# Reading 128 weight rows early, through GpSimd's queue, on 32 partitions instead of 128

## The chip, the cores and the metric

One core of one Trainium2 chip runs the program. The metric is the time of one execution on the device, in microseconds (us), as the median of three runs. One more execution was taken with the hardware profiler; its rows are shown below.

## What is computed

A decode step of one transformer block with adaptive layer norm, for a batch of 4 and a model width of 512, all in float32:

```python
x = A_x
mod = (_silu(c) @ w_mod).reshape(c.shape[0], 6, 1, -1)
sa, ca, ga, sb, cb, gb = (mod[:, 0], mod[:, 1], mod[:, 2], mod[:, 3], mod[:, 4], mod[:, 5])
h = _layernorm(x, axis=-1) * (1 + ca) + sa
x = x + ga * _A_ref(h, A_k_cache, A_v_cache, A_wq, A_wo)
h = _layernorm(x, axis=-1) * (1 + cb) + sb
x = x + gb * _B_ref(h, B_w1, B_w3, B_w2)
return x
```

`_A_ref` is attention of 32 query heads and 8 key/value heads over the last 2048 cached positions, `_B_ref` a gated feed-forward layer with 1792 inner columns. The change is about `gb`, the last of the six gates: four batch rows of `_silu(c)`, 512 long, times the last 512 columns of `w_mod`, a matrix of 512 rows.

## The kernel before

Everything that is read once from memory, some 101 MB, is streamed into two large SBUF buffers `KV[0]` and `KV[1]` and a smaller one, `WP`. Nearly all of it is loaded by one queue, SyncE's (SP): the helper `load` at L89 issues a transfer of 128 partitions, and before a buffer is overwritten SP waits for the product that last read it. The first transfers are `T0` (the condition vector `c` and the weights of the first two gates) and the caches of the first head group; ScalarE's queue adds two more (`t1_in` and the 4 rows of `x_in`). Then a loop runs over four pairs of head groups, each with its scores, softmax, values and output projection.

After the loop comes a straight part, the "post" block. The weights of three gates (`wm_in`), the first feed-forward weights (`f1_in`, `f2_in`), the weights of the last gate (`gb_in`, 1 MB, four chunks of 128 rows side by side) and the second feed-forward weights (`w2_in`, in six pieces of 1 MB, 1 MB, 512, 512, 256 and 256 KB) follow one another in SP's queue in this order, with a semaphore for each. TensorE takes them up in the same order and waits for each semaphore. A product of a 128-row chunk with the four batch rows is one call of `mm` at L255; its result is 4 rows by 512 columns in a PSUM bank. For `gb` four chunks go to four groups of rows of the bank `bM`, ScalarE copies the bank to `gb_sb`, and a product with the 0/1 matrix `same` adds the four groups. The last piece of `w2_in` is multiplied last; VectorE then forms `yt` (L488) and `y` (L490), and SP writes `out` (L492).

GpSimd does little: it clears a few tiles at the start (L128 to L139) and later passes semaphores on.

Of the kernel before, what the change touches and what calls it, by code (L numbers as in the profile page):

```python
# [5 lines left out]
AF = mybir.ActivationFunctionType  # L6
# [4 lines left out]
B, D, HQ, G, SK, DH, W, FF = 4, 512, 32, 8, 8192, 128, 2048, 1792  # L11
P = 128
# [2 lines left out]
EPS = 1e-5  # L15
CHUNKS = [(j, c) for c in range(4) for j in range(4) if c < 2 or j < 3]
HEAD = 8
W2_CUTS = [0, 4, 8, 10, 12, 13, 14]
PAIRS = G // 2

# [20 lines left out]
        return (self.sem, self.n)  # L41


def block_kernel(nc, x_in, t0_in, t1_in, kv_in, w_in, wm_in, f1_in, f2_in, gb_in, w2_in, out):
    T, v, s, gp, S = nc.tensor, nc.vector, nc.scalar, nc.gpsimd, nc.sync

    def sems(names):
        return [nc.alloc_semaphore(n) for n in names.split()]

    def sb(name, cols, rows=P):  # L50
        return nc.alloc_sbuf_tensor(name, (rows, cols), F32).ap()

    def bank(name):
        return nc.alloc_psum_tensor(name, (P, 512), F32).ap()

    (first,) = sems("first")
    A = Queue(nc, s, "act")
    V = Queue(nc, v, "dve")
    L = Queue(nc, gp, "pool")
    dx, dt0, dt1, dkv, dk, dva, dvb, dwo, dm, df1, df2a, df2b, dgb = sems("dx dt0 dt1 dkv dk dva dvb dwo dm df1 df2a df2b dgb")  # L60
    dw = sems(" ".join(f"dw{i}" for i in range(len(W2_CUTS) - 1)))
    z_ok, q_ok, p_ok, k_ok, va_ok, vb_ok, pt_ok, o_ok, ot_ok = sems("z_ok q_ok p_ok k_ok va_ok vb_ok pt_ok o_ok ot_ok")
    s_done, q_done, qt_done, pp_done, o_done, x_done, a_done, pe, last = sems("s_done q_done qt_done pp_done o_done x_done a_done pe last")
# [1 line left out]

    KV = [sb("KV0", 16384), sb("KV1", 16384)]
    WP = sb("WP", 8192)
    T0 = KV[1][:, : 16 + 4096]
    x_sb = sb("x_sb", 512, B)
    ident, same, eps = sb("ident", P), sb("same", B), sb("eps", 1)  # L70
    sc, e1, e2 = sb("sc", 16), sb("e1", 16), sb("e2", 16)
    hT, h2T = sb("hT", 16), sb("h2T", 16)
    Z = sb("Z", B * 28)
    q_sb, p_sb, o_sb, a_sb, y_sb, g_sb, u_sb, gb_sb = [sb(n, 512) for n in "q_sb p_sb o_sb a_sb y_sb g_sb u_sb gb_sb".split()]
# [10 lines left out]
    bS, bQ, bT, bP, bO, bX, bA, bM = [bank(n) for n in "bS bQ bT bP bO bX bA bM".split()]  # L85


    def load(dst, src, sem):
        S.dma_start(dst, src).then_inc(sem, 16)  # L89

    load(T0, t0_in, dt0)
    s.dma_start(WP[:, 4096:], t1_in).then_inc(dt1, 16)
# [27 lines left out]
    S.wait_ge(x_done, G)  # L120
    load(KV[1][:, :3072], f2_in[:, :3072], df2a)
    load(KV[1][:, 3072:6144], f2_in[:, 3072:], df2b)
    load(KV[1][:, 6144:8192], gb_in, dgb)
    for a, b, sem in zip(W2_CUTS[:-1], W2_CUTS[1:], dw):
        load(KV[1][:, 8192 + a * 512 : 8192 + b * 512], w2_in[:, a * 512 : b * 512], sem)


    l_eps = L.op(gp.memset(eps, EPS))  # L128
    t = L.op(gp.memset(ident, 0.0))
    L.wait(t)  # L130
# [48 lines left out]
    v_same = V.op(v.tensor_reduce(same, ident.rearrange("p (j i) -> p i j", i=32)[:, :B, :], axis=AX.X, op=ALU.add))  # L179

    A.wait((dt0, 16))
    t = A.op(s.activation(e1, T0[:, :16], AF.Exp, scale=-1.0))
    V.wait(t)
    t = V.op(v.tensor_scalar(e2, e1, 1.0, None, op0=ALU.add))
    V.wait(t)
    t = V.op(v.reciprocal(e2, e2))
    V.wait(t, (dt0, 16))
    t_sc = V.op(v.tensor_mul(sc, T0[:, :16], e2))  # L188

    A.wait((pe, 1))  # L190
    t_sa = A.op(s.copy(sa_sb, bM[32 : 32 + B, :]))
# [1 line left out]
    t = V.op(v.scalar_tensor_tensor(xs, bM[:B, :], 1.0, xc, op0=ALU.add, op1=ALU.mult))  # L193
# [60 lines left out]
    def mm(o, lhsT, rhs, start=True, stop=True):  # L254
        return T.matmul(o, lhsT, rhs, start=start, stop=stop, skip_group_check=True)  # L255
# [46 lines left out]
    T.wait_ge(V.sem, t_sc[1])  # L302
    for k in range(4):
        for i in range(2):
            ins = mm(bM[32 * i : 32 * i + B, :], sc[:, k * B : (k + 1) * B], T0[:, 16 + (2 * k + i) * 512 : 16 + (2 * k + i + 1) * 512], k == 0, k == 3)
    ins.then_inc(pe, 1)
    T.wait_ge(V.sem, t_h[1])
    for k in range(4):
        ins = T.transpose(bT[:, k * B : (k + 1) * B], h[:, k * P : (k + 1) * P], ident[:B, :B])
# [71 lines left out]
    for k in range(4):  # L381
        for i in range(3):
            at = (3 * k + i) * 512
            ins = mm(bX[32 * i : 32 * i + B, :], sc[:, k * B : (k + 1) * B], KV[0][:, at : at + 512], k == 0, k == 3)
# [3 lines left out]

    V.wait((pe, 3), t_ga)
    t = V.op(v.tensor_mul(ag, bM[:B, :], ga_sb))  # L390
    V.wait(t)
    t_x1 = V.op(v.scalar_tensor_tensor(x1, ag, 1.0, x_sb, op0=ALU.mult, op1=ALU.add, accum_out=st2[:, 0:1]))
    t_ss, t_r0, t_xc = stats(x1, t_x1, st2)
# [10 lines left out]
    for k in range(4):  # L404
        ins = T.transpose(bT[:, k * B : (k + 1) * B], h[:, k * P : (k + 1) * P], ident[:B, :B])
# [4 lines left out]
    def view(t_):  # L410
        return t_.rearrange("p (c j i) -> p c j i", c=4, j=4)
# [4 lines left out]
    for k in range(4):  # L416
        for j in range(4):
            at = 6144 + k * 2048 + j * 512
            ins = mm(bQ[32 * j : 32 * j + B, :], h2T[:, k * B : (k + 1) * B], KV[0][:, at : at + 512], k == 0, k == 3)
# [3 lines left out]
    for k in range(4):  # L423
# [5 lines left out]
        for j in range(3):  # L429
            at = k * 1536 + j * 512  # L430
            ins = mm(bA[32 * j : 32 * j + B, :], h2T[:, k * B : (k + 1) * B], KV[1][:, at : at + 512], k == 0, k == 3)
    ins.then_inc(pe, 1)
    A.wait((pe, 7))
    t = A.op(s.activation(view(eT), view(bP)[:, :, :, :B], AF.Exp, scale=-1.0))
    V.wait(t)
    t = V.op(v.tensor_scalar(dT, eT, 1.0, None, op0=ALU.add))
    V.wait(t)
    t = V.op(v.reciprocal(rT, dT))
# [7 lines left out]
    for c in range(4):  # L446
        ins = T.transpose(bS[:, c * P : c * P + 96], u_sb[:96, c * P : (c + 1) * P], ident[:96, :96])
# [3 lines left out]


    T.wait_ge(dgb, 16)
    for k in range(4):
        ins = mm(bM[32 * k : 32 * k + B, :], sc[:, k * B : (k + 1) * B], KV[1][:, 6144 + 512 * k : 6144 + 512 * (k + 1)])
    ins.then_inc(pe, 1)
    A.wait((pe, 10))
    t_gb = A.op(s.copy(gb_sb, bM))
    T.wait_ge(V.sem, t_hid[1])
    hw = view(hidT)  # L460
    w2 = KV[1][:, 8192 : 8192 + 14 * 512].rearrange("p (n m) -> p n m", n=14)
    for i in range(len(W2_CUTS) - 1):
        T.wait_ge(dw[i], 16)
        for n in range(W2_CUTS[i], W2_CUTS[i + 1]):
            jj, c = CHUNKS[n]
            if n < HEAD:
                ins = mm(bO[32 * (n % 4) : 32 * (n % 4) + B, :], hw[:, c, jj, :], w2[:, n, :], n < 4, n >= HEAD - 4)
                continue
            for j in range(4):
                ins = mm(bX[32 * j : 32 * j + B, :P], hw[:, c, jj, :], w2[:, n, j * P : (j + 1) * P], n == HEAD, n == 13)  # L470
        if i == 0:
            T.wait_ge(A.sem, t_gb[1])
            for j in range(4):
                ins = mm(bT[32 * j : 32 * j + B, :P], same, gb_sb[:, j * P : (j + 1) * P])
# [13 lines left out]
    t = V.op(v.tensor_mul(yt, bX[:, :P], gbJ))  # L488
# [8 lines left out]
def _layout(i):  # L497
    import numpy as np

    def a(t):  # L500
        return np.ascontiguousarray(t)

    k = i["A_k_cache"][:, :, SK - W :, :].reshape(B, G, NT, 512, DH)
    v = i["A_v_cache"][:, :, SK - W :, :].reshape(B, G, NT, 4, P, DH)
    k = k.transpose(1, 4, 2, 0, 3).reshape(G, P, 8192)
    v = v.transpose(1, 4, 2, 0, 3, 5).reshape(G, P, 8192)
    wm = i["w_mod"].reshape(4, P, 6, 512).transpose(1, 0, 2, 3)
    c = i["c"].reshape(B, 4, P).transpose(2, 1, 0).reshape(P, 16)
    wq = i["A_wq"].reshape(4, P, G, 512).transpose(2, 1, 0, 3).reshape(G, P, 2048)
    wo = i["A_wo"].reshape(G, R, P, D).transpose(0, 2, 1, 3).reshape(G, P, 2048)  # L510
    pairs = [[wo[2 * p], wo[2 * p + 1]] + ([wq[2 * p + 2], wq[2 * p + 3]] if p < 3 else [wo[6], wo[7]]) for p in range(4)]
    w1 = i["B_w1"].reshape(4, P, FF).transpose(1, 0, 2)
    w3 = i["B_w3"].reshape(4, P, FF).transpose(1, 0, 2)
    w2 = i["B_w2"].reshape(14, P, D)
    return {
        "x_in": a(i["A_x"].reshape(B, D)),
        "t0_in": np.concatenate([c, wm[:, :, 1::-1].reshape(P, 4096)], 1),
        "t1_in": np.concatenate([wq[0], wq[1]], 1),
        "kv_in": np.concatenate([k, v], 2),
        "w_in": np.stack([np.concatenate(p, 1) for p in pairs]),  # L520
        "wm_in": a(wm[:, :, 2:5]).reshape(P, 6144),
        "f1_in": np.concatenate([w1, w3[:, :, 1536:]], 2).reshape(P, 8192),
        "f2_in": a(w3[:, :, :1536]).reshape(P, 6144),
        "gb_in": a(wm[:, :, 5]).reshape(P, 2048),
        "w2_in": a(np.stack([w2[4 * j + c_] for j, c_ in CHUNKS], 1)).reshape(P, 14 * D),
    }

# [14 lines left out]
```

## Time and profile before

| what | value |
|---|---|
| median of three runs | 243.21 us (242.92 to 243.47) |
| the profiled execution's own time | 243.12 us |
| its span, first to last instruction | 241.8 us |
| mean granted TensorE clock, share of full speed | 0.852 |
| moved by DMA | 101.33 MB, mean 419 GB/s |
| TensorE busy | 136.2 us, 56% of the span |

The profiled execution lies 0.09 us under the median. Its own time is 1.3 us more than its span, which is what lies around the first and the last instruction. Busy shares are means over stages with different limits, so the table alone does not say what a stage waits for.

### The profile page before, as it was taken

To read this page: it belongs to the slowest core of one execution; us is meant where nothing else is said; L and a number is where in the kernel's file an instruction comes from. 1 tells how busy PE (TensorE), PEld (TensorE's weight loads), DVE (VectorE), ACT (ScalarE), POOL (GpSimd) and SP (SyncE) were. 2 spreads that over 40 slices of the span, in tenths; PEclk is the share of its full clock that TensorE was granted. 3 is DMA by queue.
4 is the path that set the end of the run, shared out by engine and by line. 5 is a ranking of instruction groups with operands and counts; after the bars stand their busy time and mean duration, and the time that the engine had idled before them with its cause. 6 is when DMAs were issued, how large, how long until landed. Compare 5 with 4: busy or idle time off the path is not lost. (4 is left out here: it accounts for less than half of the span.)

```text
span 241.8 us, 2271 instructions
## 1 busy us (share of the span) xinstructions
PE 136.2 (56%) x940; PEld 37.3 (15%) x940; DVE 38.6 (16%) x126; ACT 25.1 (10%) x54; POOL 1.7 (1%) x14
## 2 busy tenths in 40 slices
PE   3004677817660387276723772667237768665964
PEld 0000121201210012112200121112001222111211
DVE  3003202202200022022000220220002222124122
ACT  2002002100120002001100020001001201123110
POOL 2000000000000000000000000000000000000000
PEclk9999959967996579987985798879858997995999
DMA  7998989899989898999898989998989999999992
GB/s 266 451 500 369 499 371 488 379 417 445 493 379 488 369 499 381 407 428 510 369 499 369 499 369 423 434 510 369 499 350 442 442 400 440 453 431 396 418 411 106
DMA packets 4044, 101.33 MB, mean 419 GB/s; under 512 B 452, under 2 KB 580, under 8 KB 1096
## 3 DMA queue, kind: packets, MB, share of 16 engines
q1 hardware_dynamic: 3888, 99.17, 95.6%
q10 hardware_dynamic: 152, 2.11, 2.1%
q8 instruction: 3, 0.05, 0.1%
q14 instruction: 1, 0.01, 0.0%
HBM read 101.20 MB, written 0.07 MB: 419 GB/s over the span
## 5 line engine op out<-in xcount | busy, mean ns | idle before, releaser
L255 PE MATMUL bS<-KV,Z 128*16 128x512 f32 x256 | 42.5, 824 | 38.8 <-PEq L258 38.8
L255 PE MATMUL bO<-KV,pT 128*16 128x512 f32 x256 | 31.9, 642 | 0.5
L255 PEld LDWEIGHTS bS<-KV,Z 128*16 128x16 f32 x256 | 9.1, 122 | 66.6 <-issue 66.6
L218 DVE TENSOR_REDUCE MX<-bS 128x1 f32<-128x512 f32 x8 | 5.5, 691 | 79.6 <-PE bS L255 79.6
L255 PE MATMUL bM<-KV,sc 128*4 128x512 f32 x24 | 7.3, 835 | 16.6 <-DVE sc L188 16.6
L367 ACT ACTIVATE p_sb<-bS,NB 128x512 f32<-128x512 f32 x8 | 5.5, 687 | 101.2 <-ACTq L358 101.2
L276 PE MATMUL bP<-ident,p_sb 128*128 128x128 f32 x32 | 5.0, 280 | 17.3 <-PEq L258 17.3
L255 PE MATMUL bA<-WP,oT 128*4 128x512 f32 x64 | 10.4, 728 | 5.2 <-PEq L258 5.2
L255 PEld LDWEIGHTS bO<-KV,pT 128*16 128x16 f32 x256 | 8.1, 105 | 22.9 <-issue 22.9
L372 ACT ACTIVATE o_sb<-bO,LB 128x512 f32<-128x512 f32 x8 | 5.5, 687 | 48.7 <-ACTq L358 48.7
L255 PE MATMUL bQ<-WP,hT 128*4 128x512 f32 x64 | 9.2, 648 | 0.6 <-DVE hT L197 0.6
L276 PE MATMUL bX<-ident,o_sb 128*128 128x128 f32 x32 | 5.0, 280 | 7.9 <-PEq L258 7.9
L244 DVE TENSOR_REDUCE oT<-bX 128x16 f32<-128x64 f32 x8 | 1.8, 224 | 44.0 <-PE bX L276 44.0
L276 PE MATMUL bT<-ident,q_sb 128*128 128x128 f32 x32 | 5.5, 298 | 3.6 <-PEq L258 3.6
L276 PEld LDWEIGHTS bP<-ident,p_sb 128*128 128x128 f32 x32 | 3.4, 140 | 24.4 <-issue 24.4
L276 PEld LDWEIGHTS bX<-ident,o_sb 128*128 128x128 f32 x32 | 3.4, 141 | 15.0 <-issue 15.0
L227 DVE COPY pT<-bP 128x256 f32<-128x256 f32 x8 | 3.4, 424 | 13.7 <-PE bP L276 13.7
L255 PE MATMUL bQ<-KV,h2T 128*4 128x512 f32 x32 | 5.3, 831 | 0.3 <-DVE h2T L408 0.3
L276 PEld LDWEIGHTS bT<-ident,q_sb 128*128 128x128 f32 x32 | 3.7, 150 | 8.3 <-issue 8.0
L255 PEld LDWEIGHTS bM<-KV,sc 128*4 128x4 f32 x24 | 1.0, 106 | 22.6 <-DVE sc L188 18.2
L255 PE MATMUL bX<-KV,sc 128*4 128x512 f32 x24 | 4.4, 592 | 0.0
L202 DVE TENSOR_REDUCE Z<-bT 128x16 f32<-128x64 f32 x8 | 1.8, 224 | 15.4 <-PE bT L276 15.1
(101 smaller groups left out, 68.0 us busy)
## 6 DMA issues: line engine op xcount, KB each, us to landing
WP<-w_in SPq DMA_DIRECT2D x3, 4096.0 KB, 18.9
KV<-kv_in SPq DMA_DIRECT2D x1, 4096.0 KB, 24.1
KV<-f_in SPq DMA_DIRECT2D x1, 4096.0 KB, 25.9
KV<-kv_in SPq DMA_DIRECT2D x1, 3072.0 KB, 30.9
KV<-wm_in SPq DMA_DIRECT2D x1, 3072.0 KB, 16.5
KV<-f_in SPq DMA_DIRECT2D x2, 1536.0 KB, 17.2
KV<-t_in SPq DMA_DIRECT2D x1, 2056.0 KB, 12.3
WP<-t_in ACTq DMA_DIRECT2D x1, 2048.0 KB, 12.5
```

Source lines behind the costliest of these rows:

```text
L202: v.tensor_reduce(Z.rearrange("p (b i) -> p b i", b=B)[:, :, 12 : 12 + R], bT.rearrange("p (r k i) -> p i r k", r=R, k=4)[:, :B], axis=AX. ...
L218: t = V.op(v.reduce_max(MX[:, 0:1], bS, axis=AX.X))
L227: v.tensor_copy(pT.rearrange("p (t b c r) -> p c b t r", t=NT, b=B, c=4), bP.rearrange("p (c b i) -> p c b i", c=4, b=B)[:, :, :, :16].rea ...
L244: V.op(v.tensor_reduce(oT.rearrange("p (r b) -> p r b", r=R), diag, axis=AX.X, op=ALU.add), ot_ok)
L255: return T.matmul(o, lhsT, rhs, start=start, stop=stop, skip_group_check=True)
L276: ins = T.transpose(dst[:, c * P : (c + 1) * P], src[:, c * P : (c + 1) * P], ident)
L367: A.op(s.activation(p_sb, bS, AF.Exp, bias=NB[:, 0:1], accum_out=SM[:, 0:1]), p_ok)
L372: A.op(s.mul(o_sb, bO, LB[:, 0:1]), o_ok)
```

## The change

The last of the four chunks of `gb`'s weights, rows 384 to 511 of `w_mod`, leaves SP's transfer `gb_in`, which shrinks from 2048 to 1536 columns. It gets an array of its own, `gc_in`, in which the 128 weight rows lie as 32 rows of 2048 columns (four weight rows side by side, `SUB = 4`), in eight groups of four with a row of zeros behind each group. GpSimd's queue loads these 32 rows at the start of the program into a tile `GC` of 80 partitions that it has cleared before: 16 rows to partitions 16 to 31 and 16 rows to partitions 64 to 79. One transfer ahead of these two and one behind them move 16 rows of 512 bytes each into a tile `GZ` that nothing reads. The condition vector gets 16 more columns that match the new layout, so that `T0` and the tiles `sc`, `e1` and `e2` grow from 16 to 32 columns.

TensorE multiplies `GC` after the product `ag`, with four calls of `mm` over 80 partitions that write the four row groups of `bM`; later the remaining three chunks are added to three of these groups.

```diff
+SUB = 4
+BANDS = [16, 64]
+ROWS = [p for at in BANDS for p in range(at, at + 16)]
+C_IN = 16 + 4 * SUB
+W2_AT = 6144 + 1536
...
+    GC, GZ = sb("GC", SUB * 512, 80), sb("GZ", P, 96)
...
-    load(KV[1][:, 6144:8192], gb_in, dgb)
+    load(KV[1][:, 6144:7680], gb_in, dgb)
...
+    t = L.op(gp.memset(GC, 0.0))
+    L.wait(t)
+    gp.dma_start(GZ[:16], gc_in[:4, :4, :P]).then_inc(dgc, 16)
+    for e, at in enumerate(BANDS):
+        gp.dma_start(GC[at : at + 16], gc_in[4 * e : 4 * e + 4, :4]).then_inc(dgc, 16)
+    gp.dma_start(GZ[80:], gc_in[:4, :4, :P]).then_inc(dgc, 16)
...
     t = V.op(v.tensor_mul(ag, bM[:B, :], ga_sb))
+    T.wait_ge(V.sem, t[1])
+    T.wait_ge(dgc, 64)
+    for m in range(SUB):
+        mm(bM[32 * m : 32 * m + B, :], sc[:80, 16 + m * B : 16 + (m + 1) * B], GC[:, m * 512 : (m + 1) * 512], True, m == 3)
...
-    for k in range(4):
-        ins = mm(bM[32 * k : 32 * k + B, :], sc[:, k * B : (k + 1) * B], KV[1][:, 6144 + 512 * k : 6144 + 512 * (k + 1)])
+    for k in range(3):
+        ins = mm(bM[32 * k : 32 * k + B, :], sc[:, k * B : (k + 1) * B], KV[1][:, 6144 + 512 * k : 6144 + 512 * (k + 1)], False, True)
...
+    gc = np.zeros((8, 5, SUB * 512), c.dtype)
+    gc[:, :4] = i["w_mod"][384:, 5 * 512 :].reshape(SUB, 32, 512).transpose(1, 0, 2).reshape(8, 4, SUB * 512)
...
-        "gb_in": a(wm[:, :, 5]).reshape(P, 2048),
+        "gb_in": a(wm[:, :3, 5]).reshape(P, 1536),
+        "gc_in": gc,
```

On SP's queue, near its end, these transfers stood one behind the other; a row gives the line, the tile, the source, and partitions by columns:

```order
L89 DMA KV<-f_in 128x8192
L89 DMA KV<-f_in 128x3072 [waits x_done]
L89 DMA KV<-f_in 128x3072
L89 DMA KV<-gb_in 128x2048
L89 DMA KV<-w_in 128x2048 x2
L89 DMA KV<-w_in 128x1024 x2
L89 DMA KV<-w_in 128x512 x2
```

and now these stand there:

```order
L95 DMA KV<-f_in 128x8192
L95 DMA KV<-f_in 128x3072 [waits x_done]
L95 DMA KV<-f_in 128x3072
L95 DMA KV<-gb_in 128x1536
L95 DMA KV<-w_in 128x2048 x2
L95 DMA KV<-w_in 128x1024 x2
L95 DMA KV<-w_in 128x512 x2
```

Only the size of `gb_in` differs; no transfer of SP's moved past another. On GpSimd, at the start of the program, the change puts a memset and four transfers ahead of the old memsets:

```order
L556 MEMSET const-uint8-127 128x1
L134 MEMSET GC 80x2048 [waits barrier_Pool_Activation_PE_DVE_SP_gather]
L136 DMA GZ<-gc_in 16x1x128 [waits pool]
L138 DMA GC<-gc_in 16x1x2048 x2
L139 DMA GZ<-gc_in 16x1x128
L140 MEMSET eps 128x1
L141 MEMSET ident 128x128
L144 ISA [waits pool]
L144 AFFINE_SELECT ident<-ident 128x128
```

Before, the memset of `eps` was the first of GpSimd's work; all nine later instructions now come behind the four transfers. On TensorE, behind the products for the three gates, this stood (a row is a product or a transpose, with the tiles and the rows by columns of its result):

```order
L255 MATMUL bX<-KV,sc 4x512 [waits dm]
L255 MATMUL bX<-KV,sc 4x512 x11
L405 MATMUL bT<-ident,h 128x4 [waits dve]
L405 MATMUL bT<-ident,h 128x4 x3
L255 MATMUL bQ<-KV,h2T 4x512 [waits df1,dve]
```

and now this stands there:

```order
L267 MATMUL bX<-KV,sc 4x512 [waits dm]
L267 MATMUL bX<-KV,sc 4x512 x11
L267 MATMUL bM<-GC,sc 4x512 [waits dgc,dve]
L267 MATMUL bM<-GC,sc 4x512 x3
L421 MATMUL bT<-ident,h 128x4 [waits dve]
L421 MATMUL bT<-ident,h 128x4 x3
L267 MATMUL bQ<-KV,h2T 4x512 [waits df1,dve]
```

Four products came in ahead of the transposes of `h`; the four products of `bM` that wait for `dgb` further down became three.

## Rows read from the trace of the kernel before

**Rows 1.** The page, DMA and bytes in 40 slices, and its queues.

```profile
DMA  7998989899989898999898989998989999999992
GB/s 266 451 500 369 499 371 488 379 417 445 493 379 488 369 499 381 407 428 510 369 499 369 499 369 423 434 510 369 499 350 442 442 400 440 453 431 396 418 411 106
q1 hardware_dynamic: 3888, 99.17, 95.6%
q8 instruction: 3, 0.05, 0.1%
```

**Rows 2.** The chain that ended last: start us, length us, what.

```profile
212.29 26.78 DMA KV<-w_in
239.06 0.04 issue
239.11 0.45 PE bX L255 x8
...
239.57 0.30 DVE yt L488
...
239.90 0.29 DVE y L490
```

**Rows 3.** Windows at the end; the last two numbers are DMA share, GB/s.

```profile
227.80:230.27 2.47, 2.47 (x19) 0.73 (x16) 1.12 (x4) 0.22 (x1) 0.00 (x0) 1.00 1.01 421
...
235.28:236.57 1.29, 1.04 (x8) 0.11 (x8) 0.14 (x1) 0.00 (x0) 0.00 (x0) 1.00 1.01 386
236.57:237.20 0.63, 0.58 (x20) 0.35 (x23) 0.55 (x1) 0.00 (x0) 0.00 (x0) 1.00 0.76 267
237.20:238.02 0.82, 0.53 (x20) 0.24 (x20) 0.00 (x0) 0.00 (x0) 0.00 (x0) 1.00 0.18 67
238.02:238.40 0.38, 0.38 (x16) 0.17 (x8) 0.00 (x0) 0.00 (x0) 0.00 (x0) 1.00 0.12 49
238.40:238.65 0.25, 0.25 (x12) 0.11 (x8) 0.00 (x0) 0.00 (x0) 0.00 (x0) 1.00 0.11 41
238.65:239.06 0.41, 0.24 (x8) 0.00 (x0) 0.00 (x0) 0.00 (x0) 0.00 (x0) 1.00 0.00 0
```

**Rows 4.** DMA issues: KB each, median us from issue to landing.

```profile
KV<-w_in SPq DMA_DIRECT2D x2, 1024.0 KB, 23.9
KV<-gb_in SPq DMA_DIRECT2D x1, 1024.0 KB, 20.8
```

**Rows 5.** Timeline of SP's queue around the issue of gb_in.

```profile
209.44 0.43 SPq L89 DMA_DIRECT2D KV<-gb_in  x1
```

**Rows 6.** Timeline of the start: GpSimd's memsets, and what TensorE then waits for.

```profile
1.43 0.52 POOL L135 MEMSET y_sb<- 128x512 f32 x1
2.53 2.08 PE L255 MATMUL bA<-y_sb 128*128 128x512 f32 x2 [2.53 <-POOL x1J L139]
21.25 1.02 PE L255 MATMUL bM<-KV,sc 128*4 128x512 f32 x2 [16.65 <-DVE sc L188]
```

**Rows 7.** Timeline from 215 us on, where the four products come in.

```profile
216.03 0.68 DVE L390 TENSOR_TENSOR ag<-bM,ga_sb 4x512 f32<-4x512 f32 x1 [5.26 <-ACT ga_sb L387]
220.26 0.58 PE L405 MATMUL bT<-ident,h 4*128 4x4 f32 x4 [4.98 <-DVE h L398]
228.09 0.42 PEld L276 LDWEIGHTS bP<-ident,g_sb 128*128 128x128 f32 x4 [0.86 <-DMA KV<-f_in]
231.86 1.04 PE L255 MATMUL bM<-KV,sc 128*4 128x512 f32 x8
235.32 1.04 PE L255 MATMUL bO<-KV,hidT 128*4 128x512 f32 x8 [1.16 <-DMA KV<-w_in]
```

More of the change, by code (lines that the diff above doesn't have):

```diff
@@ L41, in op, with block_kernel @@
         return (self.sem, self.n)
-def block_kernel(nc, x_in, t0_in, t1_in, kv_in, w_in, wm_in, f1_in, f2_in, gb_in, w2_in, out):
+def block_kernel(nc, x_in, t0_in, t1_in, kv_in, w_in, wm_in, f1_in, f2_in, gb_in, gc_in, w2_in, out):
     T, v, s, gp, S = nc.tensor, nc.vector, nc.scalar, nc.gpsimd, nc.sync
@@ L59, in block_kernel @@
     L = Queue(nc, gp, "pool")
-    dx, dt0, dt1, dkv, dk, dva, dvb, dwo, dm, df1, df2a, df2b, dgb = sems("dx dt0 dt1 dkv dk dva dvb dwo dm df1 df2a df2b dgb")
+    dx, dt0, dt1, dkv, dk, dva, dvb, dwo, dm, df1, df2a, df2b, dgb, dgc = sems("dx dt0 dt1 dkv dk dva dvb dwo dm df1 df2a df2b dgb dgc")
     dw = sems(" ".join(f"dw{i}" for i in range(len(W2_CUTS) - 1)))
@@ L67, in block_kernel @@
     WP = sb("WP", 8192)
-    T0 = KV[1][:, : 16 + 4096]
+    GC, GZ = sb("GC", SUB * 512, 80), sb("GZ", P, 96)
+    T0 = KV[1][:, : C_IN + 4096]
     x_sb = sb("x_sb", 512, B)
     ident, same, eps = sb("ident", P), sb("same", B), sb("eps", 1)
-    sc, e1, e2 = sb("sc", 16), sb("e1", 16), sb("e2", 16)
+    sc, e1, e2 = sb("sc", C_IN), sb("e1", C_IN), sb("e2", C_IN)
     hT, h2T = sb("hT", 16), sb("h2T", 16)
@@ L122, in block_kernel @@
     load(KV[1][:, 3072:6144], f2_in[:, 3072:], df2b)
-    load(KV[1][:, 6144:8192], gb_in, dgb)
+    load(KV[1][:, 6144:7680], gb_in, dgb)
     for a, b, sem in zip(W2_CUTS[:-1], W2_CUTS[1:], dw):
-        load(KV[1][:, 8192 + a * 512 : 8192 + b * 512], w2_in[:, a * 512 : b * 512], sem)
+        load(KV[1][:, W2_AT + a * 512 : W2_AT + b * 512], w2_in[:, a * 512 : b * 512], sem)
+    t = L.op(gp.memset(GC, 0.0))
[4 more added lines that the diff above has]
+    gp.dma_start(GZ[80:], gc_in[:4, :4, :P]).then_inc(dgc, 16)
     l_eps = L.op(gp.memset(eps, EPS))
@@ L181, in block_kernel @@
     A.wait((dt0, 16))
-    t = A.op(s.activation(e1, T0[:, :16], AF.Exp, scale=-1.0))
+    t = A.op(s.activation(e1, T0[:, :C_IN], AF.Exp, scale=-1.0))
     V.wait(t)
@@ L187, in block_kernel @@
     V.wait(t, (dt0, 16))
-    t_sc = V.op(v.tensor_mul(sc, T0[:, :16], e2))
+    t_sc = V.op(v.tensor_mul(sc, T0[:, :C_IN], e2))
     A.wait((pe, 1))
@@ L304, in block_kernel @@
         for i in range(2):
-            ins = mm(bM[32 * i : 32 * i + B, :], sc[:, k * B : (k + 1) * B], T0[:, 16 + (2 * k + i) * 512 : 16 + (2 * k + i + 1) * 512], k == 0, k == 3)
+            ins = mm(bM[32 * i : 32 * i + B, :], sc[:, k * B : (k + 1) * B], T0[:, C_IN + (2 * k + i) * 512 : C_IN + (2 * k + i + 1) * 512], k == 0, k == 3)
     ins.then_inc(pe, 1)
@@ L460, in block_kernel @@
     hw = view(hidT)
-    w2 = KV[1][:, 8192 : 8192 + 14 * 512].rearrange("p (n m) -> p n m", n=14)
+    w2 = KV[1][:, W2_AT : W2_AT + 14 * 512].rearrange("p (n m) -> p n m", n=14)
     for i in range(len(W2_CUTS) - 1):
@@ L508, in _layout @@
     c = i["c"].reshape(B, 4, P).transpose(2, 1, 0).reshape(P, 16)
+    cs = np.zeros((P, SUB * B), c.dtype)
+    cs[ROWS] = i["c"].reshape(B, 512)[:, 384:].reshape(B, SUB, 32).transpose(2, 1, 0).reshape(32, SUB * B)
+    gc = np.zeros((8, 5, SUB * 512), c.dtype)
+    gc[:, :4] = i["w_mod"][384:, 5 * 512 :].reshape(SUB, 32, 512).transpose(1, 0, 2).reshape(8, 4, SUB * 512)
     wq = i["A_wq"].reshape(4, P, G, 512).transpose(2, 1, 0, 3).reshape(G, P, 2048)
@@ L516, in _layout @@
         "x_in": a(i["A_x"].reshape(B, D)),
-        "t0_in": np.concatenate([c, wm[:, :, 1::-1].reshape(P, 4096)], 1),
+        "t0_in": np.concatenate([c, cs, wm[:, :, 1::-1].reshape(P, 4096)], 1),
         "t1_in": np.concatenate([wq[0], wq[1]], 1),
```

## The prediction

> **What bounds the kernel now.** I read the chain that ended last first, because it says what the end waits for. It is one DMA: the last piece of `w_in`, issued at 212.29, on the way for 26.78 us, with only 1.1 us of TensorE and VectorE behind it [rows 2]. So no product and no vector work sets the end; a transfer queued behind other transfers does.
>
> Next the page's slices, to see whether the DMA engines ever pause. They don't: from the first slice on the busy share is 8 or 9 tenths, and one queue, SP's, fills 95.6% of the 16 engines' span [rows 1]. A byte is therefore not free because it is read early; what is read at the start pushes all that SP has queued behind it. Order alone buys nothing here.
>
> Then the end, in small windows. Up to 236.57 the share is 1.01: all 16 engines work. From 237.20 it is 0.18, from 238.02 0.12, from 238.40 0.11, then 0.00 [rows 3]. A share of 0.12 of 16 engines is 1.9 engines, and 0.11 is 1.8; 41 to 49 GB/s against 421 for all 16 (26 each) says the same. So **two engines** work on alone until 238.65, some 1.45 us after most were done at 237.20, and the last transfer lands 0.41 us later. Between 237.20 and 238.02 the share is 0.18 x 16 x 0.82 = 2.4 us of engine time; the two take 1.6 of it, so about 0.7 us is left for a third that ends near 237.9. This is the reading on which everything rests: the end is not set by the sum of the bytes but by the two engines with the most work left. What delayed them no row names. Three fetches of instructions, 0.05 MB together and so 16 KB each [rows 1], ride on the same engines and are candidates.
>
> **The change, part by part.**
>
> *SP's transfer `gb_in` loses a quarter.* It is issued at 209.44 and lands 20.8 later, at 230.2 [rows 4, 5]. The window up to that landing, 2.47 us at 421 GB/s, moves 1.04 MB, which is this 1 MB [rows 3]. A quarter is 0.62 us, on each of the 16 engines alike, since each carries 8 of the 128 partitions' rows: 16 KB, in 8 pieces of 2 KB.
>
> *The same 256 KB come back in GpSimd's queue, as 32 rows of 8 KB.* A row of 8 KB takes 2.47/8 = 0.31 us on an engine. What that does to the end depends on who moves them. Lower bound for an engine: it moves none and keeps the whole 0.62 us. If all 16 share the 32 rows, each moves two, 0.62 us, and nothing is gained. If eight share them, each of the eight moves four, 1.24 us, a net loss of 0.62 us, and the other eight keep 0.62. If four share them, those lose 1.85.
>
> *The two unread transfers* are 32 rows of 512 bytes. At 26 GB/s a row takes 0.02 us; four on one engine are 0.08 us, and none is the lower bound. How a small row compares with this rate no row shows; I take 0.08 and keep twice that for the range. `T0` grows by 64 bytes on each of 128 partitions, 8 KB in all or 0.02 us.
>
> *GpSimd's work at the start.* The memset of `GC` has 2048 columns; that of `y_sb` has 512 and takes 0.52 us [rows 6], so about 2.1 us. The issue of a transfer from GpSimd is not in the trace. It delays the nine instructions queued behind it: `eps`, `ident` and the zeroed tiles. TensorE's first product waits for the last of them at 2.53, takes 2.08, and TensorE then idles 16.65 us until `sc` [rows 6]. So the memset and four issues are free up to some 16 us, or 3.6 us for each issue; beyond that they would show in the first gate.
>
> *Four products more on TensorE, one fewer later.* They need `ag`, done at 216.71, and TensorE's next work is the transposes at 220.26, after 4.98 us of idling [rows 7]. Four such products took 1.04 us at 231.86 at a granted clock of 1.00. Even at half clock, twice that, they end at 218.8 and are free. If they ran late, the next cover is the 0.86 us wait for `f_in` at 228.09, and after it 1.16 us for `w_in` at 235.32 [rows 7]. The vector and scalar engines get nothing new on this path except 16 more columns at the start.
>
> **Sum.** For the late two, if neither moves a row of 8 KB: -0.62 + 0.08 + 0.02 = -0.52 us, and I round to -0.50 for the completion marks of four more transfers. Against the profiled execution's 243.12 that is 242.62; against the median, which is 0.09 higher, 242.71. The next in line do not hide it: most engines end by 237.20, plus 0.62 plus 0.1 is 237.9, and the late two then end at 238.15. Only the third, near 237.9, could: if it carries four rows it ends at 238.6 and eats the gain.
>
> Which engines carry the rows is what the trace does not tell. The Trainium skill, "DMA: Bandwidth & Descriptors", section on why a DMA increments its semaphore by 16, says that GpSimd's transfer runs on the largest number up to 16 that divides the slowest dimension on both sides, on consecutive engines from a cursor that goes round. By that rule a source of 4 x 4 rows runs on four engines, the first unread transfer takes engines 0 to 3, the two bands 4 to 7 and 8 to 11, and the last 12 to 15; no run here shows it yet. By the rule alone the sum is -0.50 for engines 0 to 3 and 12 to 15 and +0.64 for 4 to 11.
>
> **The rivals.**
>
> *One of the two late engines carries four of the rows.* Then the end comes later by 4 x 0.31 - 0.62 + 0.02 = 0.64 us: 243.85. For it: two late engines out of 16, eight of which would carry rows; drawn blindly both escape in only (8 x 7)/(16 x 15) = 0.23 of the draws. Against it: nothing in the rows, only that the late engines need not be a blind draw, since extra traffic such as fetches goes to fixed places. It decides as soon as one of the two late engines is among the eight. The Trainium skill, the same page, section on latency and other measured facts, says that engines 7 and 15 are usually slower; if the late two are these, 7 carries rows by the rule above and this rival holds. The trace gives two late engines, as that sentence has it, but not their numbers.
>
> *The rows are shared by all 16 engines.* Then each moves as much as before, plus two unread rows of 512 bytes and `T0`'s growth, 0.04 + 0.02 us: 243.27. For it: SP's transfers spread over all 16. Against: a source with a gap behind every four rows is not one block. The Trainium skill's section on issuing engines, in the same page, holds that another queue saves no bandwidth; the 95.6% of SP's queue agrees, and by it alone the time stays here.
>
> *A third engine becomes the last.* If the third late engine carries rows, or an instruction fetch moves ahead of an engine's last pieces because TensorE's program is 3 products longer before the end, the gain shrinks to 0.0 to 0.2 us: 243.1. For it: one window with 2.4 us of engine time where two engines explain 1.6 [rows 3].
>
> **How the numbers follow.** Between the blind 0.23 and 1 I take 0.58 for both late engines going free and nothing else in the way, about the middle; this is a judgement, the rows don't settle it. It gives 242.71, with its own range 242.5 to 242.9 for noise and the price of small rows. The first rival gets 0.26 (243.85), the even spread 0.08 (243.27), the third engine 0.08 (243.1). About 0.2%, or 0.49 us, is what a measurement of this kernel can tell from no change; the forecast of -0.50 lies on this line, so its 0.58 splits into 0.36 faster and 0.22 the same. With the two middle cases the same has 0.38, and slower 0.26. The range must leave out no more than 2 in 10: from 242.5 it goes up to the middle of the first rival, 243.85, which keeps about half of it and all the others.
>
> **What the profile after would show.** Right: a share of DMA near 0.12 that ends 0.5 us earlier than 238.65, with a higher share between 237.2 and 237.9 (eight engines with 0.6 us more); the queue of GpSimd with 136 or so packets and 0.28 MB; `w_in`'s last piece still the end of the chain; TensorE's four products between 216.7 and 219. First rival: one engine alone, share 0.06, up to about 239.2. Even spread: the same tail as before. I would be wrong altogether if `sc` or the first gate came later than 21.25, which would mean that GpSimd's issues cost more than 3.6 us each, or if TensorE no longer waited for `w_in` at the end.

## The result, and the profile after

The changed kernel takes 243.68 us (median of 20 runs, 242.79 to 243.99), the kernel before, run beside it, 243.08 (20 runs, 242.84 to 243.47): a ratio of 1.0018, 95% interval 1.0012 to 1.0025. It is slower by a little under 0.2% as a ratio and by 0.60 us between the medians; the forecast was 242.71. Two things stand out beside the median: the spread is twice that of before (1.2 us against 0.63), and 12 of the 20 runs are at 243.63 or above, while one is at 242.79, next to the forecast. The profiled execution is milder than the median: 243.38, span 242.0.

The chain that ended last, profiled execution of the changed kernel (start us, length us, what), which answers to [rows 2]:

```profile
213.03 26.27 DMA KV<-w_in
239.31 0.04 issue
239.35 0.45 PE bX L267 x8
239.79 0.02 issue
239.82 0.30 DVE yt L504
```

The same DMA ends it, 0.25 us later than in [rows 2]. Windows at the end (the last two numbers are DMA share and GB/s), which answer to [rows 3]:

```profile
235.50:236.80 1.30, 1.04 (x8) 0.11 (x8) 0.13 (x1) 0.00 (x0) 0.00 (x0) 1.00 1.00 386
236.80:237.40 0.60, 0.56 (x16) 0.32 (x16) 0.56 (x1) 0.00 (x0) 0.00 (x0) 1.00 0.84 321
237.40:238.05 0.65, 0.41 (x12) 0.11 (x8) 0.00 (x0) 0.00 (x0) 0.00 (x0) 1.00 0.36 120
238.05:238.50 0.45, 0.40 (x16) 0.32 (x16) 0.00 (x0) 0.00 (x0) 0.00 (x0) 1.00 0.13 50
238.50:238.90 0.40, 0.40 (x16) 0.11 (x8) 0.00 (x0) 0.00 (x0) 0.00 (x0) 1.00 0.05 20
238.90:239.31 0.41, 0.22 (x8) 0.00 (x0) 0.00 (x0) 0.00 (x0) 0.00 (x0) 1.00 0.00 0
```

The share between 236.8 and 238.05 is higher than before, as forecast. But the tail did not come forward. Up to 238.50 two engines work (0.13 x 16 = 2.1), from there to 238.90 one alone (0.05 x 16 = 0.8). The engine that ends last finishes 0.25 us after the 238.65 of [rows 3] where -0.50 was forecast.

The page's queues show the traffic that was added, and the start of GpSimd (timeline) what its issues cost, beside [rows 6]:

```profile
q1 hardware_dynamic: 3888, 98.91, 95.3%
q0 software_dynamic: 224, 0.28, 0.4%
```

```profile
0.74 1.80 POOL L134 MEMSET GC<- 80x2048 f32 x1 [0.29 <-POOLq L556]
2.85 0.70 POOL L136 DMA_DIRECT2D GZ<-gc_in  x1 [0.31 <-POOL GC L134]
3.54 1.11 POOL L138 DMA_DIRECT2D GC<-gc_in  x2
4.64 0.57 POOL L139 DMA_DIRECT2D GZ<-gc_in  x1
...
7.01 2.07 PE L267 MATMUL bA<-y_sb 128*128 128x512 f32 x2 [7.01 <-POOL x1J L151]
...
21.51 6.45 PE L267 MATMUL bM<-KV,sc 128*4 128x512 f32 x16 [12.43 <-DVE sc L200]
...
217.50 1.04 PE L267 MATMUL bM<-GC,sc 80*4 80x512 f32 x8 [1.48 <-DVE ag L402]
221.01 0.41 PE L421 MATMUL bT<-ident,h 4*128 4x4 f32 x4 [2.46 <-DVE h L414]
```

The memset took 1.80 us (2.1 estimated), an issue 0.56 to 0.70. TensorE still waits 12.43 us for `sc` behind them, so they are hidden. The four products run in TensorE's idle time and the transposes still wait 2.46 us for `h`. All of this is as forecast. One of the prediction's signs of being wrong altogether did come up: the first gate starts at 21.51, later than 21.25. It does not mean what the prediction read into it, issues of more than 3.6 us: `x_in` landed 0.13 us later, and the work on 32 columns in place of 16 took the rest. GpSimd's queue has 224 packets where 136 or so were expected; the last section says what they are.

The packet records of the trace say more than the page. On one engine a packet starts within some 4 ns of the end of the one before, so the packets can be strung into 16 chains, one for each engine; where two engines end a packet within a few ns of each other, the chains can be mixed up. A band is one of the two transfers of 16 rows of 8 KB. In the changed kernel's profiled execution:

- each of GpSimd's transfers has its data on four engines, a different four each time; each engine of a band has four packets of 8192 bytes at 309 ns, as forecast (0.31);
- the two late engines, those that end last, are the ones with the first two of three 16 KB instruction fetches (queue q8, at 35.2 and 214.0 us; the third, at 237.5, comes when most engines are done). Both lie in the four of the last unread transfer and carry no row of 8 KB;
- the packets of the unread transfers (four rows, 2048 bytes each; start ns, queue, bytes, ns), and below them the two fetches with the packet of SP's behind each:

```
 7125 0 2048  84      29187 0 2048 548
 7278 0 2048  84      29540 0 2048 640
 7289 0 2048  84      29711 0 2048 567
 7317 0 2048  84      29776 0 2048 664

 35179 8 16384  966     36131 1 65536 2885
213985 8 16384 1100    215071 1 32768 1681
```

A packet of 64 KB takes 2418 ns and one of 32 KB 1215, so a fetch costs its engine 966 + 467 = 1433 or 1100 + 466 = 1566 ns. In the kernel before, the same two fetches cost 1031 + 468 and 1100 + 467 ns, about the 1.45 us by which two engines work on alone [rows 3]. This names what the prediction left open: the late engines are late by their fetches.

The first transfer's packets took 84 ns, the forecast 0.08 us. The last one's took 548 to 664 ns, and SP's 64 KB packets behind them on those four engines 2580 to 2644 instead of 2418. The engine that ends last paid 0.64 + 0.16 = 0.80 us. The sum for it is now -0.62 (its quarter) + 0.80 + 0.02 (`T0`) + some 0.05 for completion marks (an estimate) = +0.25, which is the 0.25 of the chain. The other late engine paid 0.55 + 0.18 = 0.73 us and yet ended 0.42 us earlier, at 238.48, where before both ended at 238.65. Most of that comes from the start: the first packets of the engine that ends last lost 0.9 us over their usual 0.61 us each, those of the other 0.5. Such losses differ between engines and executions, so the close agreement of the sum is in part luck. It accounts for the profiled execution; whether it also accounts for the median is what the experiments had to show.

### The profile page after: what moved, and what is told of

Its sections match the earlier page's. It is cut to its first block, busy times and chain, and to the rows that moved or that the text cites. A ratio compares the mean times of both kernels' runs of the same rounds, so it can differ in the third digit from the quotient of the medians.

```text
span 242.0 us, 2289 instructions
## 1 busy us (share of the span) xinstructions
PE 139.8 (58%) x946; PEld 38.1 (16%) x946; DVE 38.8 (16%) x126; ACT 25.1 (10%) x54; POOL 5.9 (2%) x19
## 5 line engine op out<-in xcount | busy, mean ns | idle before, releaser
L267 PE MATMUL bS<-KV,Z 128*16 128x512 f32 x256 | 43.6, 843 | 37.7 <-PEq L270 37.7
L267 PE MATMUL bO<-KV,pT 128*16 128x512 f32 x256 | 33.0, 659 | 0.5
L288 PE MATMUL bP<-ident,p_sb 128*128 128x128 f32 x32 | 5.5, 298 | 17.3 <-PEq L270 17.3
L267 PE MATMUL bA<-y_sb 128*128 128x512 f32 x2 | 2.1, 1140 | 7.0 <-POOL x1J L151 7.0
```

Source lines behind the costliest of these rows:

```text
L288: ins = T.transpose(dst[:, c * P : (c + 1) * P], src[:, c * P : (c + 1) * P], ident)
```

## The experiments

**First: is it the last unread transfer?** Theory: the late two pay for its rows. Rivals: a late engine carries a band; or GpSimd's issues, the bands or the products cost the time. Three edits move that transfer or shorten it, one puts the bands on its engines instead.

```diff
 e1_mid:  -    gp.dma_start(GZ[80:], ...)           # behind the bands
          +        if p == 0:                       # in the loop, about 55 us
          +            gp.dma_start(GZ[80:], ...)
 e2_end:  +    gp.wait_ge(dw[-1], 16)               # behind w_in's last piece
          +    gp.dma_start(GZ[80:], ...).then_inc(dgd, 16)
 e3_tiny: +    gp.dma_start(GZ[80:, :4], gc_in[:4, :4, :4])
 e4_ddrr: both unread transfers ahead, bands third and fourth
```

> The last of the four GpSimd transfers, the second unread one, is issued after the load of KV[1] has landed (about 53 us) instead of behind the bands; all else is as changed. Theory 1 (in the changed kernel's trace the four rows of this transfer took 0.55 to 0.66 us on each of four engines instead of 0.08, and the packets behind them 0.16 to 0.23 more; the two late engines are among these four, so the 0.62 us that they had saved is spent there): if the price comes from the moment, 29 to 30.5 us, when SP's next load is being set up, the price falls to about 0.1 us and the time to 242.6 (ratio 0.998). Theory 1b (the price belongs to a transfer of small rows beside 64 KB rows, whenever it runs): the time stays near 243.7 (1.002). Rival (a late engine carries rows of 8 KB): moving this transfer changes nothing, 243.7.

> The second unread transfer is issued only when the last piece of w2 has landed, behind all reading, and SP waits for it at the end (semaphore of its own). Theory 1: the late engines then keep the whole saving, so the last piece lands 0.5 us earlier than before the change and the time is 242.6 (0.998), unless the wait at the very end shows. Theory 1b says the same. Rival (a late engine carries rows): 243.7 (1.002) or more. Second rival (GpSimd's queue as such costs every engine, whatever its last transfer does): 243.4.

> The second unread transfer moves 16 rows of 16 bytes instead of 512. Theory 1 with the price going by bytes: the price falls to 0.03 us and the time to 242.6 (0.998). With the price going by rows, or by the moment at which it runs: 243.5 to 243.7 (1.002), as in the changed kernel. Rival (a late engine carries rows): 243.7.

> Both unread transfers go ahead of the two bands, and the bands go to partitions 64 to 79 and 80 to 95. If the transfers run on four engines each in turn, the bands now run on engines 8 to 15 and the unread ones on 0 to 7. Theory 1 (the two late engines are among 12 to 15): each of them now carries four rows of 8 KB, so they end 0.64 us later than before the change: 243.7 to 243.8 (1.003), and the trace shows the two late engines further behind the others than before, by some 1.2 us against the engines without rows. Rival (late engines among 4 to 11, which the changed kernel loaded): a late engine in 4 to 7 would go free now, and the time would fall to 242.6 to 243.1. If the rows are shared by all engines the order changes nothing, 243.7.

Measured on one chip, before 243.07, four runs of each: e1_mid 242.82 (ratio 0.9993, 0.9979 to 1.0007), e2_end 242.70 (0.9985, 0.9971 to 1.0), e3_tiny 242.82 (0.9992, 0.9978 to 1.0007), e4_ddrr 243.66 (1.0027, 1.0013 to 1.0042). The four packets of the transfer that was moved or shortened took 84 ns each in e1_mid, 81 to 98 in e2_end, 11 to 159 in e3_tiny. The chain of e2_end:

```profile
238.72 0.04 issue
238.76 0.45 PE bX L266 x8
```

The end is 0.59 us earlier than in the changed kernel. In e4_ddrr, with the bands on the third and fourth set of four engines, it is later:

```profile
239.64 0.04 issue
239.68 0.45 PE bX L267 x8
```

That is 0.58 us behind the 239.06 of [rows 2], where the first rival has 0.64. So a late engine is among those of the third and fourth set, and its packets put it in the fourth; where a band lies on it the time is near the first rival's 243.85. At this point the unread rows looked like the whole answer.

**Second: what makes the rows dear?** The same transfer took 84 ns early and 0.6 us at 29 us.

```diff
 e5_five_at_55:     five unread transfers back to back in the loop
 e6_after_x:        all four transfers behind x_in's landing
 e7_unread_only:    the kernel before, plus
+    for at in (0, 16, 64, 80):
+        gp.dma_start(GZ[at : at + 16], gc_in[:4, :4, :P]).then_inc(dgc, 16)
 e8_again:          the changed kernel once more
 e9_one_row:   +    gp.dma_start(GY, gc_in[:4, :1, :512])   # one row of 2 KB per engine
```

> As e1, but five unread transfers of 16 rows of 512 bytes are issued one right behind the other after KV[1] has landed (about 55 us), so that every one but the first has others of GpSimd's ahead of it in the queue. Theory Q (the price comes when the transfer stands behind other GpSimd transfers that are not done): the first set of four rows takes 0.08 us an engine, the later four sets 0.5 us or more, and the late engines (12 to 15, the first and the fifth set) pay again, so the time goes back to 243.2 to 243.7. Theory M (the price comes from the moment, 8 to 30 us): all twenty sets of rows take 0.08 us each, and the time stays within 0.15 us of e1, 242.8 to 243.0.

> All four GpSimd transfers are issued only after x has landed (about 18 us), behind the memsets, with an empty queue of GpSimd's. Theory Q: the first unread set takes 0.08 us an engine although it now runs at about 21 us, the last one, behind the bands, 0.5 us or more. Theory M: the first set, at 21 us, is slow (0.5 us or more), and the last, which now runs near 40 us, takes 0.08 us; the time then is 242.6 to 242.8.

> The kernel before with only four unread transfers of 16 rows of 512 bytes added on GpSimd's queue at the start, one for each group of four engines; the last gate's weights stay in SP's transfer. This measures the disputed cost by itself. With the 0.08 us that I forecast for a set: 243.2. Theory Q or M (all sets but the first run behind others, between 8 and 12 us): the late engines pay 0.6 to 0.9 us, and the time is 243.7 to 244.0 (1.003).

> The changed kernel once more, for a second profile. If the price of the last unread transfer is what decides, its four rows take some other time than in the first profile (0.55 to 0.66 us), and the end moves with it: price on the late engines of 0.1 us means 242.7, 0.8 us 243.4, 1.2 us 243.8. If something else decides, the time does not follow the price.

> The last unread transfer moves the same bytes to the same four engines at the same place in the queue, but as one row of 2 KB for each engine and no longer as four rows of 512 bytes. If the price comes from the four short rows in one packet, the packets take about 0.08 us, the last piece lands as early as with the 16-byte rows and the time is 242.8 us. If it comes from the bytes of any packet that stands behind other transfers of GpSimd's, they take 0.5 to 0.9 us and the time stays at 243.5 to 243.7 us.

e5_five_at_55: 244.70 (1.0071, 1.0054 to 1.0088); the packets of the first of the five took 84, 84, 84 and 260 ns, those of the other four 165 to 967. That speaks against the moment and for standing behind other transfers of GpSimd's. But e6_after_x (243.19, the profiled execution alone) had 84, 206, 866 and 791 ns in its first set and 236 to 616 in its last, which neither theory foretold, and the first transfer of all, which has none of GpSimd's ahead of it, had one packet of 852 ns in e1_mid and one of 575 in e3_tiny. So neither theory holds. e7_unread_only: 244.10 (1.0041, 1.0027 to 1.0055); the first six packets took 84 ns, the other ten 466 to 888. Sixteen packets of 2 KB that nobody reads, and no band, cost 1 us:

```profile
q0 software_dynamic: 128, 0.03, 0.2%
```

e8_again (243.34, the profiled execution alone): 84, 84, 749 and 266 ns in the last set, so the price differs between executions of one kernel. One late engine paid 84 ns there and ended at 238.22; the one that ended last did so at 238.87. e9_one_row: 84, 84, 86 and 84 ns in its profiled execution (242.78), which fits "short rows in one packet", though its first set, of short rows, had 84, 84, 84 and 645; but its median is 243.66 (1.0021, 1.0012 to 1.003), and only 2 of its 11 runs are below 243.5. That fits neither expectation: the packets were cheap where they could be seen, and the time was not.

**Third: two groups of times.** Two more kernels ran beside e9_one_row, on the same chip.

```diff
 e10_end_again:     e2_end once more
 e11_no_last:
-    gp.dma_start(GZ[80:], gc_in[:4, :4, :P]).then_inc(dgc, 16)
-    T.wait_ge(dgc, 64)
+    T.wait_ge(dgc, 48)
```

> The kernel with the last unread transfer behind w_in's last piece once more, for its interval. If the late two engines paid 0.8 us for the unread rows and nothing else stands in the way, 242.6 to 242.8 us, 0.3 us under the kernel before. If the first look was luck, 243.1 us or above.

> The last unread transfer is left out and nothing else changes. If the loss is the price of its rows on the late two engines, 242.6 to 242.85 us, as with that transfer at the end; the late two then still pay for the marks of three transfers. If the loss comes from GpSimd's issues, from the bands or from the products, 243.4 us or more stay.

Both expectations failed. e10_end_again, the kernel that had taken 242.70, took 243.59 (12 runs; 1.0016, 1.0006 to 1.0026), and e11_no_last, without the blamed transfer, 243.48 (1.0009, 0.9997 to 1.0021). Their runs, in us:

```
e10  242.53 243.83 242.85 243.63 243.69 243.55 243.74 243.68 242.62 243.81 243.49 243.54
e11  242.58 243.39 243.58 242.63 243.55 243.75 243.95 242.67 243.60 242.48 243.70 243.41
```

There are two groups, a lower one, 242.5 to 242.9, and an upper one, 243.4 to 243.95, with nothing between. The first of each row is the profiled execution, in the lower group. The windows of e10_end_again's show the tail that was forecast, with no engine at work after 238.02:

```profile
236.60:237.20 0.60, 0.34 (x8) 0.04 (x8) 0.00 (x0) 0.00 (x0) 0.00 (x0) 1.00 0.82 307
237.20:238.02 0.82, 0.77 (x24) 0.43 (x24) 0.00 (x0) 0.00 (x0) 0.00 (x0) 1.00 0.35 135
238.02:238.40 0.38, 0.26 (x8) 0.00 (x0) 0.00 (x0) 0.00 (x0) 0.00 (x0) 1.00 0.00 0
```

The first theory therefore does not carry the median. A new one, C: the place from which GpSimd's transfers take their engines moves on between executions, so the bands sometimes hit the late two. Three more profiled executions of the kernel without the last transfer, which issues three transfers of four engines, and more runs of e2_end's kernel, which issues a full turn of 16, test it.

> The kernel without the last unread transfer, for its packets: it issues three transfers of four engines each. Theory C: the place from which GpSimd's transfers take their engines is kept from one execution to the next. Each execution of this kernel then moves it on by twelve engines, and the rows fall on the late two in some executions and not in others: times of either 242.5 to 242.7 or 243.4 to 243.9 us, and other engines with rows in this look than in the next two. Theory R: every execution starts at the same place, the rows lie on the same engines in all looks, and the two groups of times have another cause.

> The same once more. Theory C: the bands lie on other engines than in the look before, unless the executions between the looks add up to a full turn. Theory R: on the same.

> The same a third time, with the same expectations; over the three looks theory C expects at least one in which a late engine carries rows of 8 KB, with 243.4 us or more, and theory R none.

> The kernel with the last unread transfer at the end, which issues four transfers of four engines, a full turn of 16, behind kernels that issue three. Theory C: all its executions here lie in one group, since it leaves the place where it found it: all at 242.5 to 242.9 us, or, if it finds the place shifted, all at 243.4 to 243.9. Theory R: both groups mixed, as in its second run.

e12 to e14: 242.61, 242.70 and 242.46; in all three the late two (fetches at about 34 and 213.5) carry no band. e15_end_alone: 243.65 (12 runs, 242.40 to 243.88; 1.0013, 0.9999 to 1.0027), 4 in the lower group and 8 in the upper. Theory C in this form falls on both points: no profiled execution had the rows on other engines, and a full turn did not keep to one group. Of the 43 timed runs of e9, e10, e11 and e15 of which no packets are on record, 9 are in the lower group, a share of 0.21; the seven profiled executions of e9 to e15 are all in it. At that share seven of seven is not chance, so a profiled execution differs from the others in something that no row shows.

**Last: does the upper group go with the rows?** Theory U: in those executions an engine with four rows of 8 KB is one of the late two (the first rival; 4 x 0.31 = 1.24 us between the groups).

```diff
 e16_even:  rows with a gap behind each, over 16 engines, no unread transfer
+        gp.dma_start(GC[at : at + 16], gc_in[16 * e : 16 * e + 16, :1])
 e17_extra_8k: the kernel before, gb_in whole, plus transfers that nothing uses
+    gp.dma_start(GZ[:16], gc_in[:4, :4, :4])
+    for e, at in enumerate([16, 64]):
+        gp.dma_start(GC[at : at + 16, :2048], gc_in[4 * e : 4 * e + 4, :4, :2048])
+    gp.dma_start(GZ[80:], gc_in[:4, :4, :4])
 e18_extra_4k: the same with :1024
```

> The 32 rows of 8 KB go out over all 16 engines, two each, and there is no unread transfer. Theory U (the two groups of times differ in whether an engine with four rows is one of the late two): every engine moves as much as before, so there is one group, and it lies at 243.1 to 243.4 us, as the kernel before. Theory O (something else in the timed executions, such as GpSimd's issues or the copying of the rows): two groups 1 us apart stay.

> The kernel before, with its whole transfer of the last gate's weights, and on top four transfers that nothing uses: 16 rows of 16 bytes, two of 16 rows of 8 KB, 16 rows of 16 bytes, on four engines each. Theory U: eight engines have 4 x 0.31 = 1.24 us more to do, the other eight nothing. Where both late engines are among the others, 243.1 to 243.4 us; where one of them carries rows, 244.2 to 244.5. Two groups, 1.1 to 1.3 us apart, and the upper one the larger, as in the runs so far. Theory O: no gap of that size, or the same gap as with rows of 4 KB.

> The same with rows of half the length, 4 KB. Theory U: half the gap: 243.1 to 243.3 and 243.6 to 243.9 us. Theory O: the same gap as with 8 KB.

e17_extra_8k: 243.01 (the profiled one), 243.70, 243.90, and four at 244.31 to 244.59; median 244.31 (1.0055, 1.0042 to 1.0069). The lowest and the four highest lie where theory U had them, 1.3 to 1.6 us apart; two lie between. e18_extra_4k: 243.32 to 244.24, median 243.91 (1.0031, 1.0019 to 1.0044). One run lies at the edge of the lower of the two expected places, three at the edge of the upper (243.85 to 243.94), two above both. No clean groups show, and in the profiled execution (244.13) the 16-byte rows of the last transfer took 534, 553, 591 and 167 ns; the late engines, which carry no band here, are in that set, and their price (553 + 215 and 591 + 182 ns with the packet behind) is 0.77 us of the 1.08 by which this execution is over the kernel before. So this run does not settle the size of the gap. e16_even: 245.73 (five runs, 245.20 to 245.84; 1.0101, 1.0088 to 1.0115): one group, as theory U has it, but 2.5 us above its place. The windows of e16_even show where:

```profile
6.00:8.00 2.00, 1.82 (x2) 0.24 (x2) 0.00 (x0) 0.00 (x0) 0.00 (x0) 1.00 1.26 370
8.00:10.00 2.00, 0.00 (x0) 0.00 (x0) 0.00 (x0) 0.00 (x0) 0.00 (x0) 1.00 0.73 205
10.00:12.00 2.00, 0.00 (x0) 0.00 (x0) 0.00 (x0) 0.00 (x0) 0.00 (x0) 1.00 1.30 395
12.00:14.00 2.00, 0.00 (x0) 0.00 (x0) 0.00 (x0) 0.00 (x0) 0.00 (x0) 1.00 0.73 238
```

and of the changed kernel in the same stretches:

```profile
8.00:10.00 2.00, 1.08 (x2) 0.00 (x0) 0.00 (x0) 0.00 (x0) 0.00 (x0) 1.00 0.91 387
...
12.00:14.00 2.00, 0.00 (x0) 0.00 (x0) 0.00 (x0) 0.00 (x0) 0.00 (x0) 1.00 1.45 623
```

The bytes per second fall to about half behind each of the two transfers. Against some 420 that is (420 - 205) x 2 + (420 - 238) x 2, or 0.79 MB, 1.9 us of all 16 engines, most of the 2.5. (A window counts a packet whole where it starts, hence shares above 1, so this is rough.) SP's and ScalarE's 16 KB packets behind them took up to 1.73 us instead of 0.61. The even spread is thus worse by itself, and the run tells about the groups only by its small spread.

## Why the prediction was wrong

*What held.* The end is set by two engines that work alone, and the packets name them: those with the first two 16 KB instruction fetches, which the prediction took as candidates. The 0.31 us of a row, GpSimd's memset and issues, TensorE's products and their cover are as worked out; the quarter of `gb_in` and `T0` were not measured apart, but the sum with them fits. In all profiled executions with bands on four engines, but for e4_ddrr's, the late two escape the bands, and where the unread rows are cheap or late or left out the profiled time is 242.44 to 242.80 (ten executions), around the forecast 242.62 to 242.71. The Trainium skill, "DMA: Bandwidth & Descriptors", section on why a DMA increments its semaphore by 16, has transfers of 4 x 4 rows on four engines each, in turn; the packet records agree (four sets of four). The Trainium skill, the same page, section on latency and other measured facts, says that engines 7 and 15 are usually slower; the records do not agree, since they have both late engines in one set of four, and by the rule of the other section such a set is four consecutive engines, which 7 and 15 cannot both be in.

*The step that failed in the profiled execution* is the term "I take 0.08" for the unread rows. The first transfer paid exactly that; the last, which stands behind the bands, 0.55 to 0.66 us, and with what it did to the packet behind it 0.73 and 0.80 on the two engines that set the end. With 0.80 in its place the sum gives the profiled 243.38 to a few hundredths, in part by luck, as said above. e7_unread_only shows the price without any band: 0.9 to 1.0 us in each of its five runs.

*The step that failed for the median* is the weighing "between the blind 0.23 and 1 I take 0.58" of both late engines going free. Four kernels (e9, e10, e11, e15) in whose profiled executions the late two do not pay that price still take 243.4 to 243.95 in 34 of 43 timed runs, 0.9 to 1.3 us (between medians) above their lower group and near the first rival's 243.85; 12 of the changed kernel's 20 runs, at 243.63 to 243.99, are there too, above the 243.38 that the price alone gives. The share of runs that escape, 0.21, is close to the blind draw, 0.23. It is less than the half that would escape if only the place moved at which GpSimd's transfers start, by whole sets, since the late two share one set. That a late engine carries rows in these runs is argued from the size of the gap, from e4_ddrr, where it can be seen, and from the single groups of e7_unread_only (243.96 to 244.12) and e16_even, which have no uneven band; it is not shown, because no profiled execution of these kernels was of the upper group. The nine timed runs of e1_mid, e2_end and e3_tiny, on another chip, went from 242.63 to 243.27, none of them in the upper group, while e2_end's kernel is mixed on the two others (e10_end_again, e15_end_alone); so the chip, or the moment, may matter too, and no run tells these apart. What decides between the groups, and whether the rows or the fetches change engines, stays open.

*A better version.* e2_end took 0.9985 of before on one chip (0.9971 to 1.0), and 1.0016 and 1.0013 on two others, so no kernel here beats the one before on every chip. The even spread is no better version either: the prediction has it at 243.27, e16_even took 245.73. The lower group is about 0.5 us better than before, the upper 0.6 worse.

## What to carry to other kernels

Where the end is set by the engines with most left to do, work that is spread unevenly over engines is a draw: ask for each engine what it gains and carries, and do not take one profiled execution's placement for the others'. A few small rows are not priced by their bytes here (84 to 967 ns for the same 2 KB); move them behind the last transfer that counts, or leave them out. Look at all single times before a median: two groups in them said here what no profile did, and a first repeat on another chip overturned a theory that three experiments had borne out.

## What was not expected of the hardware

- A transfer of GpSimd's that has its data on four engines leaves packets on the other twelve as well: 224 packets on q0 are 32 of 8192 bytes, 8 of 2048, 24 of 16 and 160 of 4 bytes.
- Behind SP's 64 KB packets GpSimd's go one for one (rows at 17.0, 19.7, 22.4 and 25.1 us on one engine, a distance of 2.42 + 0.31), so four transfers issued by 5.2 us were done only after 30. `GZ`'s waits, by its tile's view in the changed kernel:

```profile
DMA to landing us min/median/max: 7.1/18.1/29.0
```

- A packet of four short rows took 84 ns or so at some places and in some executions, and anything up to 0.97 us in others, with rows of 16 bytes (11 to 159 ns in e3_tiny, 167 to 591 in e18_extra_4k) as with 512. It happened with transfers of GpSimd's ahead in the queue and without. Rows of 8 KB in the same queue kept to 307 to 359 ns on four engines, nearly all to 309, and took 309 to 1052 when all 16 engines carried them at once (e16_even). The cause is open.
